# x turned on VectorE and through DRAM instead of on TensorE, sine and cosine in PSUM, and three banks for the matmul units

## The chip, the cores and the metric

One core of one Trainium2 chip. The metric is the device time of one execution in microseconds. The engines are TensorE (PE; its weight loads, PEld, overlap with its matmuls), VectorE (DVE), ScalarE (ACT), GpSimd (POOL), and SyncE (SP), whose queue issues the DMAs. SBUF is the working memory; PSUM holds matmul results in eight banks of 2 KB a partition.

## The reference

Eight batches, eight heads, 576 positions, head size 64; everything is fp32.

```
scores = q @ k.T / 8, masked:
  heads 0-3: 0 <= rel < 32
  heads 4-7: 0 <= rel < 128 and rel % 4 == 0
attn = softmax(scores); x = attn @ v          # laid out as [batch, 576, 512]
theta = x @ w_theta                           # [576, 512]
zr, zi = x * cos(theta), x * sin(theta)
y = w_tok_r @ zr + w_tok_i @ zi               # over the 576 positions
u = x + y
out = u + max(u @ w_ch, 0)
```

The kernel keeps fp32 accuracy by splitting each operand into a high part and a remainder (`hi`, `lo`) and adding three products.

## The kernel before

**Layout.** The banded attention is done per head pair (`NP` = 4 pairs a batch). Its result is x transposed: `xf[b, pr]`, 128 channels by 576 positions. Theta is computed in five stages of positions, `STS = (4, 0, 1, 2, 3)`; stage 4 has 64 positions, the others 128. Theta comes out with positions on the partitions, so sine and cosine have to be multiplied by x with positions on the partitions too. `natural` (L713) makes this x: four fp32 transposes on TensorE (L718) for each stage, into one PSUM bank (`pxs`), which is held until both the sine's and the cosine's multiply have read it.

**One head pair.** `scores` (L438): matmuls into two PSUM banks ("s"), mask and row maximum on VectorE (L406), exponentials on ScalarE (L501), scaling by the sums on GpSimd (L507). `turn` (L511): eight VectorE block transposes (L522) of the probabilities. `pv` (L600): matmul with v (L614) into the two-bank tile "v", copied out to `xf` by ScalarE (L578); `x_split` (L582) makes high and low parts of x (L590, L594, L596).

**One theta stage.** `theta` (L669): twelve matmuls (L682) into a bank of tag "t" or "s" (table `TP`). `trig` (L722) and `cosine` (L693): for stage 4 first a copy (L741) and an addition (L743); then rounding to whole turns (ACT L746), the fraction (DVE L748), sine (ACT L754), absolute value (ACT L695), cosine (ACT L697), the two multiplies by x (DVE L760 or L767 for the sine, L702 for the cosine), and for each product the high part (ACT L641) and the low part (POOL L643) in `zsplit`.

**Units.** Per batch 16 units: eight `token` units (27 matmuls each, L804; then DVE L782, ACT L785, POOL L787) and eight `chan` units (12 matmuls each, L834; then DVE L813). All take turns over the two banks of tag "m". The outputs leave by L819.

**Order.** For the first batches (0, most of 1) the order is written out by a planner (`Order`) with ranks and costs, and pinned. From then on `phase(b, nb)` (L841) issues batch b's units in program order with the next batch's attention, and the theta stages of `nb = b + 1` among the first five remaining channel units; the tables `S_AT`, `PV_AT`, `TURN_AT`, `TURN_TH` say at which unit each head pair's step is issued. In a phase the pairs 2 and 3 of batch nb and the pairs 0 and 1 of batch nb + 1 go through `scores` and `turn`. TensorE keeps program order; on the other engines the framework's scheduler sets the order when the kernel is built.

**PSUM.** s: two banks, v: two, t, x: one each, m: two. For batches 2 to 7 `natural` alternates between x and the first half of v:

```
XP = {4: "x", 0: "v", 1: "x", 2: "v", 3: "x"}
```

Of the kernel before, what the change touches and what calls it, by code (L numbers as in the profile page):

```python
# [8 lines left out]
F32 = mybir.dt.float32  # L9
# [27 lines left out]


FG0 = {4: ("zl2", "zl6"), 0: ("zl3", "zl7"), 1: ("zh3", "zh7")}
KORD = (0, 4, 1, 5, 2, 6, 3, 7, 8)  # L40
# [8 lines left out]
TURN_AT = {2: 0, 3: 1, 4: 5}  # L49
TURN_TH = {5: 1}  # L50
TH_AT = 7
NK = 9


# [5 lines left out]
class Order:  # L60
# [13 lines left out]
    def pin(self, ins):  # L74
        if self.live:
            self.tc.keep_in_program_order(ins)
# [73 lines left out]
def build(ctx, tc, qT, kT, vw, wth, wtk, wch, maskb, ident, identb, outT):  # L150
# [3 lines left out]
    sp = ctx.enter_context(tc.tile_pool(name="soft", bufs=2))  # L154
    xp = ctx.enter_context(tc.tile_pool(name="xu", bufs=2))
    hp = ctx.enter_context(tc.tile_pool(name="hilo", bufs=1))
    gp = ctx.enter_context(tc.tile_pool(name="trig", bufs=2))
    ps_s = ctx.enter_context(tc.tile_pool(name="ps_s", bufs=2, space=PSUM))
    ps_v = ctx.enter_context(tc.tile_pool(name="ps_v", bufs=1, space=PSUM))
# [36 lines left out]
    def give(tag, n):  # L196
        if od.live:
            signal(("free", tag, n))

    def bank(tag, name):  # L200
        if tag == "v":
            n = yield from take(tag, 1)
            return ps_v.tile([128, 2 * DM], F32, tag=tag, name=name)[:, :DM], (tag, n)
# [489 lines left out]
    def cosine(b, st, f, z, kt, key, rel):  # L693
        yield "ACT", act(DM)
        pin(nc.scalar.activation(f, f, AF.Abs))  # L695
# [4 lines left out]
        px, rx = pxs[b, st]  # L700
        yield "DVE", dve(DM)
        pin(nc.vector.tensor_tensor(z, px, f, op=ALU.mult))  # L702
        signal(key)
        if kt is not None:
            yield None, ("px", b, st)
            give(*rx)
            yield from zsplit(b, kt, z, rel)
        elif rel:
            give(*rel)

    pxs = {}

    def natural(b, st, cs):  # L713
        px, rx = yield from bank("mmxxm"[st] if b == 0 else "x" if b == 1 else XP[st], f"xn{b}_{st}")
        px = px[:cs.stop - cs.start]
        yield "PE", 430
        for c in range(NC):
            pe(nc.tensor.transpose(px[:, 128 * c:128 * c + 128], xf[b, c][:, cs], idt))  # L718
        pxs[b, st] = px, rx
        signal(("xn", b, st))  # L720

    def trig(b, st):  # L722
        cs = slice(128 * st, min(128 * st + 128, S))
        R = cs.stop - cs.start
        yield None, ("th", b, st) if b else ("th0", st, 3)
        pt, rt = ths.pop((b, st))
        go(natural(b, st, cs))
        if b == 0 and st in FG0:
            K, gt = (hp.tile([128, DM], F32R, tag=t, name=f"{n}{b}_{st}").bitcast(F32) for t, n in zip(FG0[st], "Kg"))
            K = K.bitcast(I32)[:R]  # L730
# [7 lines left out]
        th = pt[:R]  # L738
        if R == 64 and b > 0:
            yield "ACT", act(DM)  # L740
            pin(nc.scalar.copy(g, pt[R:]))  # L741
            yield "DVE", dve(DM)
            pin(nc.vector.tensor_tensor(g, th, g, op=ALU.add))  # L743
            th = g
        yield "ACT", act(DM)
        pin(nc.scalar.activation(K, th, AF.Copy, scale=I2PI))  # L746
# [7 lines left out]
        table(nc.scalar.activation(g, f, AF.Sin, scale=2 * math.pi))  # L754
        if R == 128:
            go(cosine(b, st, f, f, st, ("cos", b, st), rf))
            yield None, ("xn", b, st)
            px, rx = pxs[b, st]
            yield "DVE", dve(DM)
            pin(nc.vector.tensor_tensor(g, px, g, op=ALU.mult))  # L760
            signal(("px", b, st))
            yield from zsplit(b, 4 + st, g, rg)
        else:
            yield None, ("xn", b, st)
            px, rx = pxs[b, st]
            yield "DVE", dve(DM)
            pin(nc.vector.tensor_tensor(gt[128 - R:], px, g, op=ALU.mult))  # L767
            yield from cosine(b, st, f, g, None, ("cos", b, st), rf)
            give(*rx)
            yield from zsplit(b, 8, gt, rg)  # L770

    uh, ul = {}, {}
# [1 line left out]
    def residual(b, d, g, ps, rel):  # L774
# [12 lines left out]
        pin(nc.gpsimd.tensor_tensor(ul[b, d][:, ts], x[:, ts], uh[b, d][:, ts].bitcast(F32), op=ALU.subtract))  # L787
        signal(("u", b, d, g))

    def token(b, d, g):  # L790
        yield None, ("z", b, KORD[0])
        yield None, ("wtk", g, KORD[0] // 2)
        ps, rel = yield from bank("m", f"y{b}_{d}_{g}")
        ps = ps[:, :HS]
        cs = slice(128 * d, 128 * d + 128)
        n = 0
        for kt in KORD:
            yield None, ("z", b, kt)
            yield None, ("wtk", g, kt // 2)
            zh, zl = zs[b, kt]  # L800
            wh, wl = (w[:, HS * (kt % 2):HS * (kt % 2) + HS] for w in wtks[g, kt // 2])
            yield "PE", 369
            for l, r in ((zh, wh), (zh, wl), (zl, wh)):
                pe(nc.tensor.matmul(ps, l[:, cs], r, start=(n == 0), stop=(n == 3 * NK - 1)))  # L804
                n += 1
        signal(("tk", b, d, g))
        go(residual(b, d, g, ps, rel), RANK["evacuate"])
# [13 lines left out]
    def chan(b, e, g):  # L821
        yield None, ("u", b, 0, g)
        yield None, ("wch", 0)
        ps, rel = yield from bank("m", f"c{b}_{e}_{g}")
        ps = ps[:, :HS]
        cs = slice(128 * e, 128 * e + 128)
        ts = slice(HS * g, HS * g + HS)
        n = 0
        for c in range(NC):
            yield None, ("u", b, c, g)  # L830
            yield None, ("wch", c)
            yield "PE", 369
            for l, r in ((wchs[c][0], uh[b, c]), (wchs[c][0], ul[b, c]), (wchs[c][1], uh[b, c])):
                pe(nc.tensor.matmul(ps, l[:, cs], r[:, ts], start=(n == 0), stop=(n == 3 * NC - 1)))  # L834
                n += 1
        go(finish(b, e, g, ps, rel), RANK["evacuate"])
# [166 lines left out]
```

## Time and profile before

| | |
|---|---|
| median of 3 runs | 598.66 us (597.17 to 598.66) |
| profiled execution | 597.07 us |
| its span in the trace | 595.3 us |
| mean granted TensorE clock | 0.984 |
| busy share of the span | PE 96%, PEld 87%, DVE 61%, ACT 59%, POOL 37% |
| HBM | 57.41 MB read, 9.44 MB written |

The span is what the trace covers; the 1.8 us beside it are start and end of the execution. A row of the timeline has its start, its length, the engine, the line and operation, output and input, and in brackets the idle time ahead of it with what ended it. A row that groups instructions has the busy time, the mean length in ns of one, and the idle time ahead of them.

### The profile page before, as it was taken

To read this page: it belongs to the slowest core of one execution; us is meant where nothing else is said; L and a number is where in the kernel's file an instruction comes from. 1 tells how busy PE (TensorE), PEld (TensorE's weight loads), DVE (VectorE), ACT (ScalarE), POOL (GpSimd) and SP (SyncE) were. 2 spreads that over 40 slices of the span, in tenths; PEclk is the share of its full clock that TensorE was granted. 3 is DMA by queue.
4 is the path that set the end of the run, shared out by engine and by line. 5 is a ranking of instruction groups with operands and counts; after the bars stand their busy time and mean duration, and the time that the engine had idled before them with its cause. 6 is when DMAs were issued, how large, how long until landed. Compare 5 with 4: busy or idle time off the path is not lost.

```text
span 595.3 us, 14176 instructions
## 1 busy us (share of the span) xinstructions
PE 569.7 (96%) x5584; PEld 516.9 (87%) x5584; DVE 361.6 (61%) x1132; ACT 351.1 (59%) x939; POOL 222.4 (37%) x206
## 2 busy tenths in 40 slices
PE   5997898999999999999999999999999999999997
PEld 4744787979998899889998899989998899989997
DVE  3889888855765667465566567655665656445112
ACT  1498967687535955568553974468564785266110
POOL 2229854534322532326142442316324253315220
PEclk9999599999999999999999999999999999999999
DMA  8982347404650074302641054401742023001002
GB/s 303 398 339 61 121 160 246 142 1 141 182 160 3 2 241 142 101 2 89 197 139 62 1 181 151 154 1 40 231 142 73 0 81 100 1 1 53 28 1 81
DMA packets 26866, 67.76 MB, mean 114 GB/s; under 512 B 2992, under 2 KB 3248, under 8 KB 26800
## 3 DMA queue, kind: packets, MB, share of 16 engines
q1 hardware_dynamic: 26800, 66.86, 32.9%
q8 instruction: 44, 0.72, 0.5%
q14 instruction: 22, 0.18, 0.1%
HBM read 57.41 MB, written 9.44 MB: 112 GB/s over the span
## 4 chain that ended last, share of the span: by engine, by line
PE 49%; DVE 22%; ACT 21%; issue 3%; POOL 2%; DMA 2%; SPq 0%; ACTq 0%; DVEq 0%; POOLq 0%
PE y L804 27%; DVE pt L522 9%; PE c L834 8%; PE s L465 5%; ACT P L501 5%; PE o L614 4%; PE th L682 3%; ACT K L697 3%; ACT zh L641 3%; ACT g L754 2%; ACT K L695 2%; DVE P L406 2%; DVE K L702 2%; POOL P L507 2%; ACT L754 1%
## 5 line engine op out<-in xcount | busy, mean ns | idle before, releaser
L787 POOL TENSOR_TENSOR u<-x,u 128x288 fp32r<-128x288 f32 x64 | 54.9, 858 | 184.9 <-ACT u L785 162.2
L522 DVE STREAM_TRANSPOSE pt<-P 32x288 f32<-32x288 f32 x224 | 105.1, 469 | 21.1 <-POOL P L507 18.0
L834 PE MATMUL c<-u,late_wc 128*128 128x288 f32 x768 | 111.7, 296 | 0.8 <-DVE x L813 0.5
L834 PEld LDWEIGHTS c<-u,late_wc 128*128 128x128 f32 x768 | 106.2, 188 | 4.8 <-DVE x L813 2.0
L785 ACT CAST u<-x 128x288 fp32r<-128x288 f32 x64 | 27.5, 430 | 129.3 <-DVE x L782 129.3
L804 PE MATMUL y<-wtkh,zh 128*128 128x288 f32 x288 | 90.6, 315 | 1.1 <-ACT zh L641 1.1
L804 PE MATMUL y<-wtkh,zl 128*128 128x288 f32 x288 | 86.6, 301 | 3.7 <-POOL zl L643 3.7
L804 PE MATMUL y<-wtkl,zh 128*128 128x288 f32 x288 | 86.2, 299 | 0.0
L643 POOL TENSOR_TENSOR zl<-g,zh 128x512 fp32r<-128x512 f32 x40 | 52.6, 1316 | 79.1 <-ACT zh L641 66.7
L501 ACT ACTIVATE P<-P,mx 128x64 f32<-128x64 f32 x216 | 72.1, 336 | 16.8 <-DVE mx L495 16.8
L682 PE MATMUL th<-wthh,xh 128*128 128x512 f32 x224 | 76.3, 402 | 0.0
L782 DVE TENSOR_TENSOR x<-y,x 128x288 f32<-128x288 f32 x64 | 28.7, 450 | 66.8 <-PE y L804 64.0
L804 PE MATMUL y<-late_wt_b,zh 128*128 128x288 f32 x320 | 68.1, 297 | 0.0
L804 PE MATMUL y<-late_wt_a,zh 128*128 128x288 f32 x256 | 58.0, 308 | 2.7 <-DVE x L782 2.7
L804 PEld LDWEIGHTS y<-wtkh,zh 128*128 128x128 f32 x288 | 55.4, 192 | 4.8 <-ACT zh L641 2.3
L804 PEld LDWEIGHTS y<-wtkh,zl 128*128 128x128 f32 x288 | 55.3, 192 | 4.5 <-POOL zl L643 4.5
L804 PEld LDWEIGHTS y<-wtkl,zh 128*128 128x128 f32 x288 | 55.5, 193 | 0.3 <-issue 0.3
L643 POOL TENSOR_TENSOR zl<-K,zh 128x512 fp32r<-128x512 f32 x32 | 42.0, 1312 | 36.1 <-ACT zh L641 36.1
L507 POOL TENSOR_TENSOR P<-P,sm 128x576 f32<-128x576 f32 x32 | 37.5, 1172 | 43.8 <-ACT xh L590 19.3
L804 PEld LDWEIGHTS y<-late_wt_b,zh 128*128 128x128 f32 x320 | 51.4, 189 | 0.3
L682 PEld LDWEIGHTS th<-wthh,xh 128*128 128x128 f32 x224 | 42.1, 188 | 8.3
L804 PE MATMUL y<-late_wt_b,zl 128*128 128x288 f32 x160 | 47.3, 296 | 0.0
(103 smaller groups left out, 1110.0 us busy)
## 6 DMA issues: line engine op xcount, KB each, us to landing
q<-in_qT_dram SPq DMA_DIRECT2D x32, 576.0 KB, 4.2
va<-in_vw_dram SPq DMA_DIRECT2D x30, 320.0 KB, 3.2
out_dram<-x SPq DMA_DIRECT2D x32, 288.0 KB, 2.1
k<-in_kT_dram SPq DMA_DIRECT2D x28, 304.0 KB, 4.6
vb<-in_vw_dram SPq DMA_DIRECT2D x29, 256.0 KB, 3.4
st_wtk<-in_wtk_dram SPq DMA_DIRECT2D x8, 576.0 KB, 8.8
st_wth<-in_wth_dram SPq DMA_DIRECT2D x4, 512.0 KB, 9.8
st_wch<-in_wch_dram SPq DMA_DIRECT2D x4, 512.0 KB, 4.9
```

Of the source, the lines that this page charges most:

```text
L465: pe(nc.tensor.matmul(ps[64 * e:64 * e + 64, n - g0], q[:, qb], k[:, QB * qb:QB * qb + BW], start=not masked, stop=not masked or n == g1 - 1))
L501: table(nc.scalar.activation(P[:, n], P[:, n], AF.Exp, bias=mx[:, n:n + 1], scale=SCALE, accum_out=sm[:, n:n + 1]))
L507: pin(nc.gpsimd.tensor_tensor(P, P, sm.unsqueeze(2).to_broadcast([128, NJ, BW]), op=ALU.mult))
L522: pin(nc.vector.transpose(pmats[b, pr][k0:k0 + QB, :, hh, QB * e:QB * e + QB], P[p0:p0 + QB, :, QB * o:QB * o + QB]))
L614: pe(nc.tensor.matmul(ps[64 * hh:64 * hh + 64, BW * j:BW * j + BW], v[:, 64 * hh:64 * hh + 64], pmats[b, pr][:, j, hh], start=True, stop=T ...
L643: pin(nc.gpsimd.tensor_tensor(lo, z, hi.bitcast(F32), op=ALU.subtract))
L682: pe(nc.tensor.matmul(pt, l, r, start=(n == 0), stop=(n == 3 * NC - 1)))
L782: pin(nc.vector.tensor_tensor(x[:, ts], ps, x[:, ts], op=ALU.add))
L785: pin(nc.scalar.copy(uh[b, d][:, ts], x[:, ts]))
L787: pin(nc.gpsimd.tensor_tensor(ul[b, d][:, ts], x[:, ts], uh[b, d][:, ts].bitcast(F32), op=ALU.subtract))
L804: pe(nc.tensor.matmul(ps, l[:, cs], r, start=(n == 0), stop=(n == 3 * NK - 1)))
L834: pe(nc.tensor.matmul(ps, l[:, cs], r[:, ts], start=(n == 0), stop=(n == 3 * NC - 1)))
```

## The change

It concerns batches 2 to 7, and the units of batches 1 to 7.

- x with positions on the partitions is no longer made by TensorE. `x_turn` transposes the 32 x 32 blocks of each `xf[b, c]` (128 x 576) on VectorE, issued after the pair's `pv`. What is left is a shuffle of whole blocks: `x_store` writes them with four DMAs to a DRAM tile (runs of 512 bytes), issued at unit 4, and `x_load` reads the rows back with five DMAs into the same SBUF space, issued at unit 6. The multiplies read this x (`by_x`).
- The cosine is written to PSUM (two halves of "v", alternating over the stages), the sine into the theta bank that it was computed from; the multiplies read it there.
- The units use three banks in turn (m, m, x) instead of two.
- The context's scratch for software DMAs is set to 1024 bytes.

```diff
-XP = {4: "x", 0: "v", 1: "x", 2: "v", 3: "x"}
+STORE_AT, LOAD_AT = 4, 6
...
     def cosine(b, st, f, z, kt, key, rel):
...
-        table(nc.scalar.activation(f, f, AF.Sin, scale=-2 * math.pi, bias=halfpi[:f.shape[0]]))
+        cs = f
+        if b > 1 and COS_PSUM:
+            if st == STS[0]:
+                cos_at[b] = yield from bank("v", f"cos{b}")
+            cs = cos_at[b][0][:f.shape[0], DM * (STS.index(st) % 2):][:, :DM]
+        table(nc.scalar.activation(cs, f, AF.Sin, scale=-2 * math.pi, bias=halfpi[:f.shape[0]]))
...
-        pin(nc.vector.tensor_tensor(z, px, f, op=ALU.mult))
+        by_x(b, st, z, cs)
...
+    def x_turn(b, c):
+        if c == 0:
+            t = cp.tile([128, 5 * DM], F32, tag="xn", name=f"xq{b}")[:, :NC * S]
+            xq[b] = t.rearrange("p (a c s) -> p a c s", c=NC, s=QB)
+        pin(nc.vector.transpose(xq[b][:, :, c], xf[b, c].rearrange("p (a s) -> p a s", s=QB)))
+
+    def x_store(b):
+        xq[b], t = dp.tile([S, DM], F32, tag="xd", name=f"xd{b}"), xq[b]
+        to = xq[b].rearrange("(a s) (g f) -> s a g f", s=QB, g=4)
+        for g in range(4):
+            pin(nc.sync.dma_start(to[:, :, g], t[QB * g:QB * g + QB].rearrange("p a c s -> p a (c s)")))
+
+    def x_load(b):
+        xn = cp.tile([128, 5 * DM], F32, tag="xn", name=f"xn{b}").rearrange("p (a d) -> p a d", d=DM)
+        for st in STS:
+            R = 64 if st == 4 else 128
+            pin(nc.sync.dma_start(xn[:R, st], xq[b][128 * st:128 * st + R]))
+            xns[b, st] = xn[:R, st].rearrange("p (g c d) -> p c g d", g=4, c=NC)
+
+    def by_x(b, st, z, f):
+        if b > 1:
+            z, f = (t.rearrange("p (c g d) -> p c g d", c=NC, g=4) for t in (z, f))
+            pin(nc.vector.tensor_tensor(z, xns[b, st], f, op=ALU.mult))
+        else:
+            pin(nc.vector.tensor_tensor(z, pxs[b, st][0], f, op=ALU.mult))
 
     def natural(b, st, cs):
+        if b > 1:
+            return
...
-        table(nc.scalar.activation(g, f, AF.Sin, scale=2 * math.pi))
+        sn = th0 if b > 1 and SIN_PSUM else g
+        table(nc.scalar.activation(sn, f, AF.Sin, scale=2 * math.pi))
...
+    def unit_bank(b, n):
+        return "mmx"[n % 3] if b else "m"
...
     def phase(b, nb):
...
+            for p in range(NP):
+                if PV_AT[p] == n and nb > 1:
+                    x_turn(nb, p)
+            if n == STORE_AT and nb > 1:
+                x_store(nb)
+            if n == LOAD_AT and nb > 1:
+                x_load(nb)
             n += 1
```

More of the change, by code (lines that the diff above doesn't have):

```diff
@@ L39 @@
 FG0 = {4: ("zl2", "zl6"), 0: ("zl3", "zl7"), 1: ("zh3", "zh7")}
+COS_PSUM, SIN_PSUM = True, True
 KORD = (0, 4, 1, 5, 2, 6, 3, 7, 8)
@@ L156, in build @@
     hp = ctx.enter_context(tc.tile_pool(name="hilo", bufs=1))
+    dp = ctx.enter_context(tc.tile_pool(name="dram", bufs=2, space=bass.MemoryType.DRAM))
     gp = ctx.enter_context(tc.tile_pool(name="trig", bufs=2))
@@ L202, in bank @@
             n = yield from take(tag, 1)
-            return ps_v.tile([128, 2 * DM], F32, tag=tag, name=name)[:, :DM], (tag, n)
+            return ps_v.tile([128, 2 * DM], F32, tag=tag, name=name), (tag, n)
         pl, bufs = banks[tag]
@@ L696, in cosine @@
         yield "ACT", act(DM) + 90
[L697 removed]
+        cs = f
[4 more added lines that the diff above has]
+        table(nc.scalar.activation(cs, f, AF.Sin, scale=-2 * math.pi, bias=halfpi[:f.shape[0]]))
         signal(("sin", b, st))
         yield None, ("xn", b, st)
[L700 removed]
         yield "DVE", dve(DM)
[L702 removed]
+        by_x(b, st, z, cs)
         signal(key)
         if kt is not None:
[L705 to L706 removed]
+            if b < 2:
+                yield None, ("px", b, st)
+                give(*pxs[b, st][1])
             yield from zsplit(b, kt, z, rel)
@@ L709, in cosine @@
             give(*rel)
-    pxs = {}
+    pxs, cos_at = {}, {}
+    xq, xns = {}, {}
+    def x_turn(b, c):
[20 more added lines that the diff above has]
+            pin(nc.vector.tensor_tensor(z, pxs[b, st][0], f, op=ALU.mult))
     def natural(b, st, cs):
-        px, rx = yield from bank("mmxxm"[st] if b == 0 else "x" if b == 1 else XP[st], f"xn{b}_{st}")
+        if b > 1:
+            return
+        px, rx = yield from bank("mmxxm"[st] if b == 0 else "x", f"xn{b}_{st}")
         px = px[:cs.stop - cs.start]
@@ L737, in trig @@
         g = gt[:R]
-        th = pt[:R]
+        th = th0 = pt[:R]
         if R == 64 and b > 0:
@@ L757, in trig @@
             yield None, ("xn", b, st)
-            px, rx = pxs[b, st]
             yield "DVE", dve(DM)
-            pin(nc.vector.tensor_tensor(g, px, g, op=ALU.mult))
+            by_x(b, st, g, sn)
+            if b > 1:
+                give(*rt)
             signal(("px", b, st))
@@ L764, in trig @@
             yield None, ("xn", b, st)
-            px, rx = pxs[b, st]
             yield "DVE", dve(DM)
-            pin(nc.vector.tensor_tensor(gt[128 - R:], px, g, op=ALU.mult))
+            by_x(b, st, gt[128 - R:], sn)
             yield from cosine(b, st, f, g, None, ("cos", b, st), rf)
-            give(*rx)
+            if b < 2:
+                give(*pxs[b, st][1])
             yield from zsplit(b, 8, gt, rg)
@@ L792, in token @@
         yield None, ("wtk", g, KORD[0] // 2)
-        ps, rel = yield from bank("m", f"y{b}_{d}_{g}")
+        ps, rel = yield from bank(unit_bank(b, NC * g + d), f"y{b}_{d}_{g}")
         ps = ps[:, :HS]
@@ L823, in chan @@
         yield None, ("wch", 0)
-        ps, rel = yield from bank("m", f"c{b}_{e}_{g}")
+        ps, rel = yield from bank(unit_bank(b, NC * (2 + g) + e), f"c{b}_{e}_{g}")
         ps = ps[:, :HS]
@@ L989 @@
     host = _arrays({n: _np.asarray(a) for n, a in inputs.items()})
-    nc = _bacc.Bacc("TRN2", target_bir_lowering=False, num_devices=1)
+    nc = _bacc.Bacc("TRN2", target_bir_lowering=False, num_devices=1,
+                     dynamic_dma_scratch_size=1024)
     arrays, args = {}, []
```

## The prediction

> **What bounds the kernel now.** I read the page first (busy shares, groups, DMA), then the length of one batch, then the chain of waits, and last the engines' timelines through one batch. In steady state one "phase" runs the token and channel units of batch b while batch b+1 is prepared; five phases (b = 1 to 5) are alike, and b = 6 has no softmax work two batches ahead of it any more.
>
> ```profile
> PE 569.7 (96%) x5584; PEld 516.9 (87%) x5584; DVE 361.6 (61%) x1132; ACT 351.1 (59%) x939; POOL 222.4 (37%) x206
> ...
> 344.89:413.78 68.89, 67.83 (x677) 63.05 (x677) 42.93 (x155) 42.23 (x121) 24.34 (x24) 1.00 0.32 105
> ...
> 317.00:345.00 28.00, 27.76 (x171) 24.75 (x171) 16.35 (x37) 20.62 (x47) 10.41 (x10) 1.00 0.01 1
> ```
>
> The columns of the stage rows are: stretch, length, then busy us of PE, PEld, DVE, ACT, POOL, the clock, the DMA share. A phase takes about 68.7 us and TensorE shows 67.8 of it busy, so at first sight only TensorE counts: what is taken off it is gained. The chain of waits says otherwise:
>
> ```profile
> 353.33 1.20 PE o L614 x36
> ...
> 386.47 3.10 ACT P L501 x18
> 390.73 1.17 POOL P L507
> 395.80 0.69 DVE g L743
> ...
> 413.78 3.46 PE c L834 x24
> ```
>
> From 353.33 to 413.78, 60 us of that 69 us phase, the chain never touches TensorE. It goes: exponentials (L501) on ScalarE, scaling by the sums (L507) on GpSimd, block transposes of the probabilities (L522) on VectorE, the next pair's mask and maximum, its exponentials, and so on through four head pairs; then the trigonometry of the five theta stages, up to 413.78, where a channel unit on TensorE has to wait for a PSUM bank that VectorE empties (L813) behind its trigonometry. In the other phases the chain shown runs over TensorE in the first half and joins this one at the last pair, so the two loops have nearly the same length. That is my main reading: **two loops tie**, and the change shortens only one of them directly.
>
> How long is the second loop by itself? One turn of it, by VectorE's timeline:
>
> ```profile
> 288.43 3.86 DVE L522 STREAM_TRANSPOSE pt<-P 32x288 f32<-32x288 f32 x8
> ...
> 323.04 3.85 DVE L522 STREAM_TRANSPOSE pt<-P 32x288 f32<-32x288 f32 x8 [1.58 <-POOL P L507]
> 326.92 0.68 DVE L743 TENSOR_TENSOR g<-th,g 64x512 f32<-64x512 f32 x1
> ...
> 357.10 3.37 DVE L522 STREAM_TRANSPOSE pt<-P 32x288 f32<-32x288 f32 x7
> ```
>
> and ScalarE's rows between:
>
> ```profile
> 327.63 0.63 ACT L746 ACTIVATE K<-g 64x512 int32<-64x512 f32 x1 [5.11 <-DVE g L743]
> ...
> 335.18 0.63 ACT L641 CAST zh<-K 128x512 fp32r<-128x512 f32 x1 [0.28 <-DVE K L702]
> ...
> 347.38 0.62 ACT L641 CAST zh<-K 128x512 fp32r<-128x512 f32 x1 [0.76 <-DVE K L702]
> 347.98 0.62 ACT L641 CAST zh<-g 128x512 fp32r<-128x512 f32 x1
> 348.62 1.28 ACT L501 ACT_TABLE_LOAD   x1
> 350.76 0.35 ACT L501 ACTIVATE P<-P,mx 128x64 f32<-128x64 f32 x1 [0.86 <-DVE mx L495]
> ...
> 353.86 0.43 ACT L785 CAST u<-x 128x288 fp32r<-128x288 f32 x1
> ```
>
> 288.43 to 357.10 is 68.67. The pieces: first to last probability transposes 38.46 (288.43 to 326.89); to the first rounding 0.74 (327.63); the trigonometry 20.97 (to 348.60); the table load 1.30 (to 349.90); a gap of 0.86, which is the only place where TensorE's scores set the pace; exponentials 3.10 (350.76 to 353.86); then 3.24 to the next transposes. Without the gap the loop is 67.8. Theta of stage 4 is copied out long before: ScalarE then sits idle 5.11 us because L743 is queued behind L522 on VectorE.
>
> In a sentence by itself: the Trainium skill, page "Trainium Kernel Development and Optimization", section "Best Practices", says that matmul busy time is not the measure of how near TensorE is to its limit, and that the busy share of the weight loads is; by that the engine stands at 87% and not at 96%.
>
> **The change part by part.** *Removed from TensorE:* the four fp32 transposes of x for each of five stages in batches 2 to 7, 30 stages in all. The undisturbed price stands in the last theta stretch:
>
> ```profile
> 524.43 1.58 PE c L834 x12
> 526.01 0.44 PE xn L718 x4
> 526.45 2.74 PE th L682 x12
> ```
>
> 0.44 a stage, 2.2 us a phase, 13.2 us in all. *Third bank:* units no longer wait for one of two banks. The waits on TensorE's weight loads from 207 to 560:
>
> ```profile
> PEld y L804 <- DVE x L782: 3.2, 4, 1.0
> ...
> PEld c L834 <- DVE x L813: 2.0, 5, 0.4
> PEld xn L718 <- PE c L834: 1.4, 4, 0.4
> ```
>
> Together 6.6 us over five phases, 1.3 a phase, which goes with the transposes' own bank waits. TensorE's own loop falls from 68.7 to 68.7 - 2.2 - 1.3 = 65.2. That is a floor and not the time, because the other loop stands at 67.8.
>
> *Added to VectorE:* four block transposes a phase, 128 x 576 each. The trace has only L522's form:
>
> ```profile
> L522 DVE STREAM_TRANSPOSE pt<-P 32x288 f32<-32x288 f32 x224 | 105.1, 469 | 21.1 <-POOL P L507 18.0
> ```
>
> If time goes by columns, 2 x 0.469 = 0.94; if four times the partitions and twice the columns cost no more than one such instruction, 0.47. I take 0.94, since the 288 columns at 0.469 already stand at 1.6 ns a column. VectorE has room for 3.8 us (43 of 69 busy); the question is what queues behind each. An x transpose can run once the copy of x out of PSUM (L578) is done, so their places are:
>
> ```profile
> 295.70 0.46 DVE L782 TENSOR_TENSOR x<-y,x 128x288 f32<-128x288 f32 x1 [2.40 <-PE y L804]
> 303.56 0.69 DVE L596 TENSOR_TENSOR xh<-x,xh 128x512 fp32r<-128x512 f32 x1
> 309.53 1.19 ACT L578 COPY x<-o 128x576 f32<-128x576 f32 x1
> 311.66 3.85 DVE L522 STREAM_TRANSPOSE pt<-P 32x288 f32<-32x288 f32 x8 [1.90 <-POOL P L507]
> ```
>
> The second falls into the idle 2.40 before 295.70: nothing. The fourth is ready at 310.72 and fits into the 1.90 before 311.66: nothing. The first becomes ready just before the 288.43 transposes; with TensorE ahead, the mask work beside it moves earlier, so I take 0, at most 0.94. The third lands among the splits near 303.5 with the next pair's mask and maximum, its exponentials and its transposes queued behind, and no slack up to the trigonometry: 0.94. Sum on the loop 0.94, bounds 0 and 1.88.
>
> *x through DRAM:* four stores, then five loads that wait for them, on SP's queue.
>
> ```profile
> q1 hardware_dynamic: 26800, 66.86, 32.9%
> ...
> out_dram<-x SPq DMA_DIRECT2D x32, 288.0 KB, 2.1
> 311.80 0.33 SPq L218 DMA_DIRECT2D q<-in_qT_dram  x1
> ...
> 344.90 4.34 SPq L819 DMA_DIRECT2D out_dram<-x  x4
> 330.24 0.68 DVE L767 TENSOR_TENSOR g<-xn,g 64x512 f32<-64x512 f32 x1 [1.26 <-ACT g L754]
> ```
>
> Behind the waiting stores on SP stand at most the loads of the next pair, issued at 311.80 and so no later than now; after them come the output stores of 344.90, and the DMA share from 317 to 345 is 0.01, so nothing collides. The transfer of 1.18 MB goes out in runs of 512 bytes, 2304 of them, 144 on each of 16 engines. Lower bound: the 2.1 of an output store. Upper: each run costs as much as a mean packet of the queue, 0.329 x 595.3 x 16 / 26800 = 0.117 us, so 16.8. I take 8. The loads, 1.18 MB again but in runs of 2048 bytes, I put at 5: above the 2.1 of one 288 KB store, below four of these in a row, 8.4. From 311.7 that is 325, before the first use at 330.24; with the store's upper bound 333.5, 3.3 late. Nothing on the path, bounds 0 and 3.3. If x came late, VectorE would stall at L767 with the whole trigonometry behind it.
>
> *Sine and cosine in PSUM:* the multiplies still read one operand from PSUM and one from SBUF, so L760 and L702 keep their 0.68. ScalarE writes PSUM in ten instructions a phase. No row shows such a write; the nearest shows the reading side:
>
> ```profile
> L695 ACT ACTIVATE K<-K 128x512 f32<-128x512 f32 x32 | 20.2, 631 | 0.9
> L746 ACT ACTIVATE K<-th 128x512 int32<-128x512 f32 x32 | 18.7, 585 | 2.7 <-PE th L682 2.5
> ```
>
> So 0 to 46 ns each, 0 to 0.46 a phase; I take 0.2. The Trainium skill, page "ScalarE: Activation LUTs", section "Step-by-step: what each stage is for", says PSUM is the quicker destination for ScalarE, without a figure; no run so far shows it, and by it the sum would take the 0.46 end. The theta bank is held until the sine is multiplied: the second half of the next scores then waits for stage 3's L760, which in the old order ended at 347.94. That is no loss while the loop ends there anyway, but it stops TensorE from running further ahead than one scores block.
>
> The smaller DMA scratch adds no instruction.
>
> *Order of the multiplies:* today L702 (cosine) goes ahead of L760 (sine) although the sine is ready 1.3 us sooner, and ScalarE waits 0.27 three times and 0.76 once for it (1.57 a phase). With x already in SBUF nothing ties the sine's multiply to TensorE. The order on VectorE is a scheduler's, so I take 1.0 of the 1.57. Of the gap of 0.86 I take half, 0.43, as the last L813 stand ahead of the masks.
>
> **The sum.** A steady phase: 68.67 + 0.94 - 1.0 - 0.2 - 0.43 = 67.98, so -0.7, times five = -3.5. The phase of b = 6 has no softmax loop and runs on TensorE: -2.2, of which I leave 0.5 for z parts coming late: -1.7. Units alone at the end: no change. Together -5.2 on the profiled 597.07 (span 595.3): 591.9. The runs' median is 1.6 above the profiled one: **593.5**.
>
> **Rivals.** *TensorE is the bound after all* (0.18). If all of 0.86, 1.57 and 0.46 comes and no x transpose is on the loop, it is 65.8, beside the floor 65.2: 5 x -2.9 - 2.2 = -16.7, so 582 in the runs' terms; if L743 also gets ahead of L522, the floor: 579. For: 67.8 of 68.7 busy. Against: the 5.11 us wait, a VectorE order that holds in all steady phases. *Nothing gained* (0.17). The order stays, only the gap goes and the x transpose eats it: 68.67 - 0.86 + 0.94 = 68.75; 597.3 with the last phase. *VectorE takes it back: slower* (0.15). Two x transposes stand ahead of L522 and the masks, no wait goes: 68.67 + 1.88 - 0.43 = 70.1; 5 x 1.45 - 1.7 = +5.6, so 604. It decides from about 0.9 us a phase on the loop that nothing repays. For: no slack between 303.5 and 327. Against: idle spots of 2.40 and 1.90. *x comes late* (0.07): 3.3 a phase at the upper bound, 5 x 2.6 - 1.7, about 610. For: small runs; against: an idle DMA.
>
> **How the numbers follow.** My forecast has 0.43, its own range 588 to 597. The range 580 to 604 leaves out the far ends of the first and the last two rivals. This kernel's measurement tells 0.3%, 1.8 us. Faster by that: most of the forecast (0.38), the TensorE case (0.18), a little of "nothing" (0.04): 0.60. Same: 0.12 + 0.05 = 0.17. Slower: 0.15 + 0.07 and a tail: 0.23.
>
> **What would show it.** Right: no L718 rows after batch 1; phases near 68; TensorE idle ahead of scores, released by the sine's multiply; the chain on L522, L501 and the trigonometry in every steady phase. The x transposes show their own rate and place. Wrong: phases of 65 to 66 with TensorE on the whole chain (the loops did not tie, or the order broke the second); L743 or L767 waiting for a DMA; ScalarE writes of sine slower than 630 ns.

## The result, and the profile after

The changed kernel takes **583.52 us** (median of 4 runs, 583.05 to 584.45), the kernel before 598.11 on the same chip: a ratio of 0.976, 95% interval [0.974, 0.978], or 14.6 us less. The forecast was 593.5. The profiled execution took 583.05, its span 581.3, at a mean granted TensorE clock of 0.988 (0.984 before).

The page of the changed kernel: busy time by engine, and the chain's shares by engine. Line numbers have moved: transposes of the probabilities L522 are L525 now, exponentials L501 are L504, rounding L746 is L787, multiplies by x L748, x transposes L729.

```profile
PE 553.6 (95%) x5464; PEld 502.7 (86%) x5464; DVE 378.0 (65%) x1156; ACT 344.3 (59%) x939; POOL 222.6 (38%) x206
...
DVE 32%; PE 29%; ACT 26%; POOL 6%; issue 4%; DMA 2%; SPq 1%; ACTq 0%; DVEq 0%; POOLq 0%
```

TensorE still shows 95% busy, yet it holds only 29% of the chain. Stage rows (stretch, length, then busy us of PE, PEld, DVE, ACT, POOL, clock, DMA share, GB/s): first a steady phase and the last phase of the kernel before, then the same two of the changed one.

```profile
279.95:348.62 68.67, 67.91 (x684) 63.07 (x680) 42.72 (x155) 42.19 (x121) 24.35 (x24) 1.00 0.32 106
485.93:550.34 64.41, 64.41 (x607) 60.87 (x607) 32.28 (x96) 36.53 (x85) 23.17 (x23) 1.00 0.13 43
```

```profile
277.99:344.27 66.28, 65.28 (x658) 60.86 (x658) 45.38 (x158) 40.91 (x120) 24.36 (x23) 1.00 0.47 145
474.16:536.44 62.28, 62.28 (x587) 58.69 (x587) 35.64 (x101) 36.34 (x86) 24.58 (x24) 1.00 0.29 87
```

A steady phase lost 2.4 us and the last one 2.13; 5 x 2.4 + 2.1 = 14.1 is the whole gain (the two profiled executions are 14.0 apart). One turn of the second loop, by VectorE's timeline and then ScalarE's, of the changed kernel:

```profile
284.29 3.87 DVE L525 STREAM_TRANSPOSE pt<-P 32x288 f32<-32x288 f32 x8
...
319.02 3.85 DVE L525 STREAM_TRANSPOSE pt<-P 32x288 f32<-32x288 f32 x8 [1.58 <-POOL P L510]
...
350.56 0.94 DVE L525 STREAM_TRANSPOSE pt<-P 32x288 f32<-32x288 f32 x2
```

```profile
323.62 0.63 ACT L787 ACTIVATE K<-g 64x512 int32<-64x512 f32 x1 [5.11 <-DVE g L784]
...
342.21 0.62 ACT L644 CAST zh<-K 128x512 fp32r<-128x512 f32 x1 [0.75 <-DVE K L748]
342.85 1.28 ACT L504 ACT_TABLE_LOAD   x1
344.27 0.35 ACT L504 ACTIVATE P<-P,mx 128x64 f32<-128x64 f32 x1
```

By the prediction's own pieces:

| piece of one turn | before | after | difference | predicted |
|---|---|---|---|---|
| first to last probability transposes | 38.46 | 38.58 | +0.12 | +0.94 |
| to the first rounding | 0.74 | 0.75 | +0.01 | 0 |
| trigonometry | 20.97 | 19.21 | -1.76 | -1.2 |
| table load | 1.30 | 1.30 | 0 | 0 |
| gap before the exponentials | 0.86 | 0.14 | -0.72 | -0.43 |
| exponentials to the next transposes | 6.34 | 6.29 | -0.05 | 0 |
| sum | 68.67 | 66.27 | -2.40 | -0.7 |

All three terms missed on the same side. The third **x transpose** of a phase on VectorE, the group of all of them, and the first one as it stands in the chain of waits:

```profile
294.85 0.76 DVE L729 STREAM_TRANSPOSE xq<-x 128x576 f32<-128x576 f32 x1
295.54 3.83 DVE L525 STREAM_TRANSPOSE pt<-P 32x288 f32<-32x288 f32 x8
```

```profile
L729 DVE STREAM_TRANSPOSE xq<-x 128x576 f32<-128x576 f32 x24 | 18.6, 773 | 9.9 <-ACT x L581 9.9
```

```profile
282.01 0.78 DVE xq L729
```

0.77 each instead of the 0.94 taken. The third stands directly ahead of the next probability transposes, as forecast. From this pair's exponentials to the next pair's (289.45 to 302.19) it is 12.74, against 12.08 before (294.12 to 306.20): +0.66. But the pair ahead of it is shorter, 11.46 instead of 12.01. ScalarE's rows there, before and after:

```profile
293.25 0.43 ACT L785 CAST u<-x 128x288 fp32r<-128x288 f32 x1 [5.99 <-DVE x L782]
293.59 0.63 ACT L578 COPY x<-o 128x576 f32<-128x576 f32 x1
294.12 0.35 ACT L501 ACTIVATE P<-P,mx 128x64 f32<-128x64 f32 x1
```

```profile
287.37 0.64 ACT L581 COPY x<-o 128x576 f32<-128x576 f32 x1 [4.68 <-DMA k<-in_kT_dram]
289.11 0.43 ACT L828 CAST u<-x 128x288 fp32r<-128x288 f32 x1 [1.11 <-DVE x L825]
289.45 0.35 ACT L504 ACTIVATE P<-P,mx 128x64 f32<-128x64 f32 x1
```

Before, the copy of x out of PSUM stood between the unit's cast and the exponentials, though ScalarE had idled 5.99 us ahead of them. Now it runs first, in that idle time, and 0.55 us comes off the loop. That repays most of the third transpose.

The first x transpose is on the chain too, in every steady phase. It costs nothing against the kernel before, because VectorE waited in that place for the next pair's scores (0.84 us ahead of the masks at 286.50). From the exponentials to the transposes of the probabilities it is 6.30 us now (277.99 to 284.29) and was 6.32 (282.11 to 288.43).

**x through DRAM** came in time. SyncE's issues of the changed kernel, and the first use of x:

```profile
307.57 3.78 SPq L736 DMA_DIRECT2D xd<-xq  x4
...
315.41 2.50 SPq L742 DMA_DIRECT2D xn<-xd  x5
```

```profile
326.82 0.68 DVE L748 TENSOR_TENSOR g<-xn,th 64x512 f32<-64x512 f32 x1 [0.85 <-ACT th L796]
```

A load takes 4.9 us to land (median), so the last is there at about 322.8, 4 us before the first use. That use waits for the sine (`th L796`), not for x.

**Writes to PSUM.** ScalarE's cosine and sine, before (first fence) and after; the columns are busy us, mean ns, idle before:

```profile
L697 ACT ACTIVATE K<-K,halfpi 128x512 f32<-128x512 f32 x32 | 23.1, 722 | 0.8
L754 ACT ACTIVATE g<-K 128x512 f32<-128x512 f32 x32 | 20.1, 629 | 3.8 <-DVE K L748 3.2
```

```profile
L705 ACT ACTIVATE cos<-K,halfpi 128x512 f32<-128x512 f32 x24 | 16.5, 687 | 0.1
L796 ACT ACTIVATE th<-K 128x512 f32<-128x512 f32 x24 | 14.3, 597 | 1.9 <-DVE K L789 1.9
```

35 and 32 ns less each, 0.33 us a phase over ten. The Trainium skill, page "ScalarE: Activation LUTs", section "Step-by-step: what each stage is for", says that ScalarE is faster to PSUM than to SBUF; these rows agree.

The largest share of the 1.76 is **ScalarE's order**. Its waits for VectorE or GpSimd in the trigonometry fell only from 1.58 us (0.28, 0.27, 0.27, 0.76) to 1.27 (0.27, 0.25, 0.75). What changed is how closely its instructions follow each other. Two stretches of it, before and after:

```profile
336.43 0.63 ACT L754 ACTIVATE g<-K 128x512 f32<-128x512 f32 x1
337.10 0.63 ACT L695 ACTIVATE K<-K 128x512 f32<-128x512 f32 x1
```

```profile
338.69 0.60 ACT L796 ACTIVATE th<-K 128x512 f32<-128x512 f32 x1
339.22 0.61 ACT L644 CAST zh<-K 128x512 fp32r<-128x512 f32 x1
339.73 0.63 ACT L698 ACTIVATE K<-K 128x512 f32<-128x512 f32 x1
340.26 0.61 ACT L644 CAST zh<-g 128x512 fp32r<-128x512 f32 x1
```

Sine and absolute value of one stage use one tile in turn and start 0.67 us apart; absolute value and cosine 0.66. The two casts and the next sine started 0.60 and 0.65 apart (335.18, 335.78, 336.43), right behind VectorE's two multiplies and fraction, which run end to end (334.45, 335.06, 335.66). With another stage's instruction between two that depend on each other they start 0.51 to 0.53 apart. In the trigonometry of a phase 3 starts before and 14 after come within 0.56 us of the one ahead. 11 x 0.15 would be 1.6 us; writes and waits leave 1.76 - 0.33 - 0.31 = 1.1 for it. That split is worked out from the rows; no run changes ScalarE's order alone. The Trainium skill, page "ScalarE: Activation LUTs", section "What ACT_TABLE_LOAD costs", gives about 93 ns by which activations in a row overlap; here that is so (0.60 busy, 0.51 apart) only where the neighbours do not share a tile.

The changed kernel's chain also runs over GpSimd's low parts inside the trigonometry, in four of the five steady phases. The chain of the kernel before holds none of them there:

```profile
333.23 3.82 POOL zl L646 x3
```

What a faster low part would give was not tried.

### The profile page after: what moved, and what is told of

Same layout as the page of the kernel before. It is cut to its first block, busy times and chain, and to the rows that moved or that the text cites. A ratio compares the mean times of both kernels' runs of the same rounds, so it can differ in the third digit from the quotient of the medians.

```text
span 581.3 us, 13989 instructions
## 1 busy us (share of the span) xinstructions
PE 553.6 (95%) x5464; PEld 502.7 (86%) x5464; DVE 378.0 (65%) x1156; ACT 344.3 (59%) x939; POOL 222.6 (38%) x206
## 4 chain that ended last, share of the span: by engine, by line
DVE 32%; PE 29%; ACT 26%; POOL 6%; issue 4%; DMA 2%; SPq 1%; ACTq 0%; DVEq 0%; POOLq 0%
DVE pt L525 14%; PE y L850 13%; ACT P L504 10%; PE c L880 7%; PE th L685 4%; DVE P L409 4%; POOL zl L646 3%; DVE xh L599 2%; POOL P L510 2%; ACT zh L644 2%; PE s L468 2%; ACT K L698 2%; ACT K L787 2%; ACT cos L705 2%; ACT th L796 2%
## 5 line engine op out<-in xcount | busy, mean ns | idle before, releaser
L525 DVE STREAM_TRANSPOSE pt<-P 32x288 f32<-32x288 f32 x224 | 104.9, 468 | 12.5 <-POOL P L510 8.9
L880 PE MATMUL c<-u,late_wc 128*128 128x288 f32 x768 | 108.9, 295 | 0.0
L685 PE MATMUL th<-wthh,xh 128*128 128x512 f32 x224 | 75.0, 396 | 5.4 <-DVE g L748 5.2
L504 ACT ACTIVATE P<-P,mx 128x64 f32<-128x64 f32 x216 | 72.1, 335 | 13.1 <-DVE mx L498 12.4
L685 PEld LDWEIGHTS th<-wthh,xh 128*128 128x128 f32 x224 | 42.0, 188 | 15.2 <-PE c L880 4.8
L581 ACT COPY x<-o 128x576 f32<-128x576 f32 x32 | 29.6, 924 | 28.7 <-PE o L617 23.9
```

The costliest lines, as they stand in the source:

```text
L504: table(nc.scalar.activation(P[:, n], P[:, n], AF.Exp, bias=mx[:, n:n + 1], scale=SCALE, accum_out=sm[:, n:n + 1]))
L525: pin(nc.vector.transpose(pmats[b, pr][k0:k0 + QB, :, hh, QB * e:QB * e + QB], P[p0:p0 + QB, :, QB * o:QB * o + QB]))
L581: pin(nc.scalar.copy(dst, src))
L685: pe(nc.tensor.matmul(pt, l, r, start=(n == 0), stop=(n == 3 * NC - 1)))
```

## The experiments

Theory 1 is the prediction's: TensorE's loop and the second loop (VectorE, ScalarE, GpSimd) nearly tie, and the change shortens the second by its order of multiplies, PSUM writes and gap, the first by transposes and bank waits. The rivals are that TensorE was the only bound, and that the third bank, or sine ahead of cosine, alone explains the gain. NOSYNC in the diffs stands for a dependency of order only. The period is that of the third steady phase, from one table load of the exponentials to the next; "against" is the median less 583.52 (the first four and the last five rows) or less the kernel before on the same chip (the middle four). The kernel before took 598.11 us where the changed one was timed, and 597.06 to 598.01 on the chips of these runs.

| version | median us | against | period |
|---|---|---|---|
| changed, units on two banks | 591.00 | +7.5 | 67.78 |
| changed, sine and cosine in SBUF | 594.73 | +11.2 | 68.63 |
| changed, cosine's multiply first | 588.01 | +4.5 | 67.20 |
| changed, half of TensorE's transposes back | 588.63 | +5.1 | 67.01 |
| before, sine's multiply first | 598.60 | +0.7 | 68.93 |
| before, one x a batch | 597.01 | 0.0 | 68.42 |
| the same, third bank | 591.54 | -6.1 | 68.32 |
| before, last transposes spread | 594.23 | -2.8 | 67.97 |
| changed, second x transpose twice | 584.37 | +0.9 | 66.27 |
| changed, third twice | 580.11 | -3.4 | 65.57 |
| changed, third twice, order held | 586.04 | +2.5 | 66.70 |
| changed, order held | 583.88 | +0.4 | 66.26 |
| changed, last transposes spread | 578.01 | -5.5 | 65.03 |

### Undoing one part of the change

**Two banks.**

```diff
     def unit_bank(b, n):
-        return "mmx"[n % 3] if b else "m"
+        return "m"
```

> The changed kernel with its third bank undone: the units of batches 1 to 7 take turns over the two banks of tag m again. Theory 1 (the loop over VectorE, ScalarE and GpSimd sets a steady phase at 66.28 us, TensorE has about 1 us of idle time in it): the bank waits come back, 0.6 to 1.0 us a phase, and fall mostly into that idle time: 0 to +2 us on 583.5. Theory 2 (TensorE sets the end): 5.2 us of bank waits come back: +4 to +5.

591.00 us, ratio to before 0.9887 [0.9863, 0.9911]: 7.5 us worse than the changed kernel, more than either theory gave. TensorE's weight loads over the whole span:

```profile
PEld c L880 <- DVE x L859: 6.8, 5, 1.4
PEld y L850 <- DVE x L825: 6.6, 5, 1.5
```

Both waits are absent from the changed kernel. The gap before the exponentials is 0.96 instead of 0.14, and ahead of it the masks wait for TensorE's scores (348.73, 0.28 us), which come behind units that waited 1.13 for a bank. The stretch from the exponentials' table load to the sine's is 49.6 us instead of 48.3, so the head pairs pay for a bank that VectorE empties late. The third bank works on the second loop and not on TensorE's alone.

**Sine and cosine in SBUF.**

```diff
-COS_PSUM, SIN_PSUM = True, True
+COS_PSUM, SIN_PSUM = False, False
```

> The changed kernel with sine and cosine written to SBUF again, so that both operands of the multiplies by x lie in SBUF. Theory 1: ScalarE loses 10 x 33 ns a phase (599 to 632, 687 to 723), and the multiplies, which run beside GpSimd's low parts, stretch as the SBUF-only subtraction at L599 does (1.64 us beside GpSimd, 0.68 without): 1 to 3 us a phase, +5 to +15 us. Theory 2: 0, since TensorE does the same work and its theta banks come free sooner.

594.73 us, ratio to before 0.995 [0.9931, 0.9969]. The multiplies by x in this run:

```profile
L748 DVE TENSOR_TENSOR g<-xn,g 128x512 f32<-128x512 f32 x24 | 29.6, 1235 | 4.3 <-ACT g L796 4.2
...
L748 DVE TENSOR_TENSOR K<-xn,K 128x512 f32<-128x512 f32 x24 | 26.7, 1111 | 5.0 <-ACT K L705 4.4
```

With both operands in SBUF a multiply takes 1.1 to 1.2 us; with one in PSUM it took 0.68. These are means. Two single ones of one phase, while GpSimd is idle and while its low parts run:

```profile
333.96 0.68 DVE L748 TENSOR_TENSOR g<-xn,g 128x512 f32<-128x512 f32 x1
...
337.19 1.71 DVE L748 TENSOR_TENSOR g<-xn,g 128x512 f32<-128x512 f32 x1
```

Once x has left PSUM, putting sine and cosine there is not an extra: without it 11.2 of the 14.6 us are gone. The Trainium skill, page "GPSIMD Engine Reference", section "8. Key points", says that GpSimd contends with VectorE instructions that have two SBUF inputs; this agrees.

**Cosine's multiply first**, as before the change:

```diff
-    xq, xns = {}, {}
+    xq, xns, by_cos = {}, {}, {}
...
-            pin(nc.vector.tensor_tensor(z, xns[b, st], f, op=ALU.mult))
+            ins = nc.vector.tensor_tensor(z, xns[b, st], f, op=ALU.mult)
+            if st < 4 and (b, st) in by_cos:
+                tc.add_manual_dep(ins.ins, by_cos[b, st].ins.name, NOSYNC, reason="cosine first")
+            by_cos[b, st] = ins
```

> The changed kernel with one thing held: on VectorE the cosine's multiply of a stage goes ahead of the sine's, as in the kernel before. Theory 1: the trigonometry, now 19.20 us, gets most of the 1.57 us of waits back: +1.0 to +1.6 a phase, +5 to +8 us. Theory 2: 0.

588.01 us, ratio 0.9823 [0.9793, 0.9853]: 0.92 us a phase, a little under theory 1. The first exponential of this run:

```profile
348.93 0.35 ACT L504 ACTIVATE P<-P,mx 128x64 f32<-128x64 f32 x1 [0.78 <-DVE mx L498]
```

The gap before the exponentials is back, 0.78 instead of 0.14. With 0.32 more from the sine's table load to the exponentials' that is the 0.92 (0.04 come off elsewhere): the order of the multiplies acts mostly through this gap. The masks wait for nothing here; they follow the sine's multiply and two additions.

**Half of TensorE's transposes back**, into the theta bank ahead of its matmuls, unused:

```diff
+        if b > 1:
+            w = min(128, S - 128 * st)
+            for c in range(2):
+                pe(nc.tensor.transpose(pt[:w, 128 * c:128 * c + 128], xf[b, c][:, 128 * st:128 * st + w], idt))
```

> The changed kernel with two fp32 transposes of x put back on TensorE ahead of every theta stage of batches 2 to 7; they write into the theta bank and theta overwrites them, so nothing waits for them and nothing uses them. Half of what the change took off: 0.22 a stage, 1.1 us a phase, 6.6 in all. Theory 1: 1.0 of each 1.1 falls into TensorE's idle time in the five steady phases, all of it shows in the last: +1 to +3. Theory 2: +6 to +7.

588.63 us, ratio 0.9846 [0.9827, 0.9865]; 0.73 us a phase, between the two theories. The stage row:

```profile
277.58:344.59 67.01, 66.56 (x669) 61.92 (x666) 45.73 (x160) 41.42 (x120) 24.32 (x24) 1.00 0.48 144
```

TensorE's work grew by 66.56 - 65.28 = 1.28 and the period by 0.73. The difference came out of its wait for the theta bank (1.0 us in this phase of the changed kernel, 0.4 here). The 0.73 shows as 0.35 in the trigonometry and 0.42 in the gap before the exponentials, now 0.56 (0.04 come off elsewhere). So TensorE has 0.5 to 0.6 us of room after the change: the two loops still nearly tie, one step lower.

### One part alone, in the kernel before

**Sine's multiply first:**

```diff
...
+        if (b, st) in sins_at:
+            tc.add_manual_dep(ins.ins, sins_at[b, st].ins.name, NOSYNC, reason="sine first")
...
```

> The kernel before with one thing held: on VectorE the sine's multiply of a stage goes ahead of the cosine's in batches 2 to 7. Theory 1 (two loops tied): the second loop falls by 1.0 to 1.6 us a phase, TensorE's stays near 68: -0.5 to -3 us on 598. Rival 3 (the order of the multiplies is most of the gain by itself): -5 to -8.

598.60 us, ratio 1.0016 [1.0001, 1.0032]; theory 1 had -0.5 to -3. Its stage row:

```profile
279.04:347.97 68.93, 67.85 (x678) 63.04 (x678) 43.24 (x154) 41.66 (x120) 24.29 (x24) 1.00 0.32 106
```

The trigonometry did shrink, from 20.97 to 20.55 us, and nothing came of it: the gap before the exponentials grew from 0.86 to 1.52. Ahead of it the masks wait for TensorE's scores, here as in the kernel before, whose row is this:

```profile
349.13 0.22 DVE L406 CUSTOM_DVE_ANT_0 P<-s,mskb 128x64 f32<-128x64 f32 x1 [0.28 <-PE s L465]
```

The scores come no sooner than TensorE's last 24 unit matmuls let them.

**One x a batch**, which takes work off TensorE:

```diff
     def natural(b, st, cs):
+        if b > 1 and st != STS[0]:
+            pxs[b, st] = pxs[b, STS[0]]
+            return
+        if b > 1:
+            cs = slice(0, 128)
...
```

> The kernel before, with one turned tile of x in each of the batches 2 to 7: positions 0 to 127 are turned on TensorE and all five stages multiply by that tile, so four of the five sets of turns are left out, with them the multiplies by the right x in stages 1 to 4; the cosine's multiply is held ahead of the sine's as it stands before. This takes about 1.76 us a phase off TensorE and nothing off the second loop but what of the 0.86 gap TensorE alone had caused. Two loops that tie (theory 1): -2 to -4.5 us, that is 0.4 to 0.9 a phase. TensorE alone sets the period (rival): -9 us, all of the 1.76 in each of five phases.

597.01 us, ratio 0.9983 [0.9964, 1.0002]: nothing that can be told, at most 2.1 us by the interval, where theory 1 expected 2 to 4.5. Stage row, TensorE's wait in it, and the exponentials:

```profile
279.73:348.15 68.42, 66.05 (x662) 61.36 (x660) 42.67 (x154) 41.72 (x120) 24.34 (x24) 1.00 0.32 106
```

```profile
PE c L844 <- DVE x L823: 1.9, 1, 1.9
```

```profile
350.73 0.35 ACT L501 ACTIVATE P<-P,mx 128x64 f32<-128x64 f32 x1 [1.29 <-DVE mx L495]
```

TensorE has 1.86 us less to do and spends it waiting for a unit's bank. The phase is 0.25 shorter. TensorE as the only bound falls. The run did not relieve TensorE alone, though: the scheduler's order changed with it, and the trigonometry is 20.27, 0.70 less. The gap took that up. It grew to 1.29, and the masks wait 0.28 for the scores here too. So TensorE's scores do set the gap, as the prediction read it, but not by TensorE's load.

What sets them is the same in the kernel before, with sine first and here. VectorE empties a unit's bank inside its trigonometry, TensorE's last 24 unit matmuls start (344.89, 344.91, 344.85), and the first exponential follows 5.87, 5.86 and 5.88 us later, behind these matmuls, the scores and the masks. This path crosses from one loop to the other over the two banks. What lies beside it, the end of the trigonometry or TensorE's transposes, can shrink without a gain.

**The same with the third bank**, the one x kept in the output's bank (the diff beside that of the run above):

```diff
-XP = {4: "x", 0: "v", 1: "x", 2: "v", 3: "x"}
+XP = {4: "v"}
...
-        ps, rel = yield from bank("m", f"y{b}_{d}_{g}")
+        ps, rel = yield from bank("mmx"[(NC * g + d) % 3] if b else "m", f"y{b}_{d}_{g}")
...
-        ps, rel = yield from bank("m", f"c{b}_{e}_{g}")
+        ps, rel = yield from bank("mmx"[(NC * (2 + g) + e) % 3] if b else "m", f"c{b}_{e}_{g}")
```

> The kernel before with one turned tile of x in each of the batches 2 to 7, as in the run that took 1.76 us a phase off TensorE (four of five sets of turns left out, stages 1 to 4 multiply by the wrong x), and besides that tile kept in the output's bank and the units of batches 1 to 7 on three banks in turn; the order of the instructions on each engine is that run's. What it tells apart is what the third bank is worth when TensorE has room and nothing else of the change is made. Third bank as the prediction sized it (it ends TensorE's waits for banks, and lets the scores come on time; the second loop keeps its length but for the 0.76 before the exponentials): 67.6 to 67.8 a phase, -3 to -4 us against that run. Banks emptied in VectorE's order hold TensorE in the second loop (the +1.5 a phase that the changed kernel lost on two banks): 66.7 to 67.2 a phase, -6 to -9 us. Units' banks play no part before the change: 0.

591.54 us, ratio 0.9889 [0.9861, 0.9918]. By medians 5.5 us less than without the bank, by profiled executions 2.5 (594.82 and 592.31); the four later periods are 67.8 to 68.3. By the profiles the five phases give 1.4 us together and the last one 1.3, less than either expectation; by the medians it lies between them. The second loop by itself is near 68 us in the old order, and the bank, worth 1.5 us a phase after the change, has little to give under it. At the end of the phase a gap of 0.77 stays, and VectorE's rows show its cause:

```profile
346.34 0.68 DVE L767 TENSOR_TENSOR g<-xn,g 128x512 f32<-128x512 f32 x1
346.94 0.81 DVE L823 SCALAR_TENSOR_TENSOR x<-c,x 128x288 f32<-128x288 f32 x2
347.66 0.21 DVE L406 CUSTOM_DVE_ANT_0 P<-s,mskb 128x64 f32<-128x64 f32 x1
```

The masks follow without a pause behind the sine's multiply and two additions; TensorE's scores are already there (346.19 to 347.46). In the changed kernel the sine's multiply is done before the cosine's, and that gap is the one that came back with cosine's multiply first.

**Last transposes spread.** The eight transposes of the last pair (L522) stand in one block of 3.85 us, with L743 queued behind them; here two of them follow each stage's fraction:

```diff
-TURN_TH = {5: 1}
+TURN_TH = {5: 4}
...
+            if pr == 1 and (b - 1, i // 2) in fracs:
+                tc.add_manual_dep(ins.ins, fracs[b - 1, i // 2].ins.name, NOSYNC, reason="late turn")
```

> The kernel before, with nothing changed but the place of the last pair's eight transposes of probabilities on VectorE: two behind the fraction of each theta stage, as in the version of the changed kernel where this gave 5.5 us. Theory 1 (the second loop then gets ahead and TensorE, busy 67.8 of 68.7 us in a phase, is left as the bound): -3 to -5 us, no more than the 0.9 a phase that TensorE idles. Were the second loop the only bound, as in the changed kernel: -5 to -8 us.

594.23 us, ratio 0.9938 [0.9916, 0.9959]; -2.8 us, just short of theory 1's -3 to -5. The phase is 67.97, 0.70 shorter, with TensorE busy for 67.44 of it, and the chain is 71% TensorE's. This is the run that relieves the second loop alone, and it shows how near the two loops were.

### The price of the x transposes

The second or the third of the four block transposes is made twice:

```diff
+        if c == 2:
+            nc.vector.transpose(xq[b][:, :, c], xf[b, c].rearrange("p (a s) -> p a s", s=QB))
```

> The changed kernel with the second x transpose of each batch done twice (0.77 us more on VectorE a phase, in a place with 1.29 us of idle time behind it). Theory 1: 0 to +0.5. Rival 4 (VectorE's load as such counts): +3.9.

> The changed kernel with the third x transpose of each batch done twice (0.76 us more on VectorE a phase, ahead of the next pair's masks, with nothing idle behind it up to the trigonometry). Theory 1: +0.76 in each of five phases, +3 to +4. Theory 2 (TensorE sets the end): 0. Rival 4 (load as such): +3.9 as for the second.

The second doubled (c == 1): 584.37 us, ratio 0.9779 [0.9755, 0.9803], period unchanged. It is free. The third doubled: 580.11, ratio 0.9711 [0.9688, 0.9734], faster. That is not the price of anything, as VectorE's rows show:

```profile
320.13 1.43 DVE L525 STREAM_TRANSPOSE pt<-P 32x288 f32<-32x288 f32 x3 [1.67 <-POOL P L510]
321.60 0.68 DVE L786 TENSOR_TENSOR g<-th,g 64x512 f32<-64x512 f32 x1
322.31 2.41 DVE L525 STREAM_TRANSPOSE pt<-P 32x288 f32<-32x288 f32 x5
```

The scheduler's order changed: stage 4's addition (L786 here) slipped between the last pair's transposes, and the trigonometry begins sooner. So the run was repeated with that addition held behind all eight transposes, beside a control with the same hold and nothing doubled:

```diff
...
+            if b + 1 in lasts:
+                tc.add_manual_dep(ins.ins, lasts[b + 1].ins.name, NOSYNC, reason="after the transposes")
...
```

> The changed kernel with the third block transpose of x made twice in each of the batches 2 to 7, and the addition of theta's last stage held behind all eight transposes of the last pair, where the changed kernel has it. Theory 1 (this transpose stands on VectorE's path from the last exponentials to the next sines): +0.77 us a phase, +3 to +4 us against the changed kernel with the same hold. Rival (it lies in VectorE's idle time): 0.

> The changed kernel with the same hold of the addition and nothing doubled. Its order on VectorE is the changed kernel's around the last transposes, so 0 (within 1 us) against it by each theory; it is what the doubled one is compared with.

586.04 (ratio 0.9805 [0.9786, 0.9824]) against 583.88 (0.9772 [0.975, 0.9793]): 2.2 us, 0.44 a phase, short of the 3 to 4 expected. The pair with the doubled transpose takes 0.68 longer, and the next one makes up 0.23. The third is on the loop, at a little over half its length. Between the two doubled runs, 580.11 and 586.04, the place of stage 4's addition is worth 5.9 us.

### A version that beats both

The same spreading of the last transposes, in the changed kernel (the diff is that of the kernel before):

> The changed kernel with the eight block transposes of the last head pair (L525) held back: two behind the fraction (L789) of each of the stages 0 to 3, instead of all eight ahead of L784. Theory 1: the trigonometry starts up to 4.4 us sooner in each steady phase, the loop over VectorE and ScalarE falls below TensorE's, and TensorE sets the phase at its busy 65.3: 5 x -1.0, about 578.5. Theory 2 (TensorE sets the end already): 0.

**578.01 us** (577.66 to 578.08), ratio to before 0.9671 [0.9653, 0.9689]. Its stage row, and the chain by engine:

```profile
273.91:338.94 65.03, 65.03 (x658) 60.83 (x656) 45.48 (x158) 41.98 (x121) 24.29 (x24) 1.00 0.50 148
```

```profile
PE 80%; DVE 9%; ACT 5%; DMA 2%; issue 2%; POOL 1%; SPq 0%; DVEq 0%; ACTq 0%; POOLq 0%
```

TensorE has no idle time left in the phase and the chain is TensorE's. This is the floor that the prediction gave for TensorE's own loop, 65.2.

## Why the prediction was right and wrong

**Two loops tie: held.** Relieving the second loop alone gave 0.70 a phase and then TensorE held it (594.23). Less work for TensorE gave 0.25 a phase (597.01), a shorter end of the trigonometry nothing (598.60); the change took 2.4. What the sum left out is the path over the two banks that ties the loops to each other. The prediction's own chain shows it, where a channel unit waits at 413.78 for a bank behind the trigonometry. The rival "TensorE is the bound after all" named the right size (582) with the wrong cause: its chain should have been TensorE's, and it holds 29%. Its sum for the second loop, 65.8 if everything comes, was the better one.

**The step that failed is the sum for the second loop**, -0.7 a phase where -2.40 came:

- *x transposes, +0.94 taken.* The place was right (the third) and 0.66 showed there; each takes 0.77 instead of 0.94. That is 0.28 of the error of 0.82. The rest is a gain of 0.55 that was not looked for: the copy of x ahead of the exponentials left the loop.
- *Order of the multiplies and PSUM writes, -1.2 taken, -1.76 measured.* The sum is nearer than its terms. Sine ahead of cosine gives 0.32 in the trigonometry (taken: 1.0), the writes up to 0.33 (taken: 0.2). The rest, about 1.1, was missed: ScalarE's own instructions close up. The prediction counted the waits shown in brackets; the 0.1 to 0.15 us that a start loses behind a neighbour it depends on stands in no bracket.
- *The gap, -0.43 taken, -0.72 measured.* It was put down to TensorE's scores, of which half was to go. Two things hold it, and either alone keeps it. On two banks the scores come late (0.86 before, 0.96 in the changed kernel with two banks). On three banks the scores are there in time, but in the old order the masks stand behind the sine's multiply (0.78). Only with both gone is it 0.14.

**The third bank** was counted for TensorE's loop only, 1.3 a phase there and nothing in the sum. Putting it back to two cost 1.5 a phase, of which 0.82 is the gap. It belongs to both loops, since VectorE empties the banks in its own order. Its place in the second loop's sum was a term put at nothing.

**What held:** -1.7 for the last phase was -2.13; x through DRAM in time (15.2 us from the first store's issue to the last landing where 13 were taken, and 4.0 us before the first use instead of 5.2); the second x transpose shown free, the fourth not on the chain, and the first on it but at no cost. The longer hold of the theta bank became TensorE's new wait, about 1.0 us once in a phase, though ahead of theta's matmuls and not of the scores:

```profile
PE th L685 <- DVE g L748: 5.2, 5, 1.2
```

**What stays open.** The parts' losses when undone (1.5, 2.4, 0.92, 0.73 a phase) add up to far more than 2.4; each is a loss of the whole arrangement, so no split of the 14.6 us by parts is given. Why the scheduler put ScalarE's copy and casts into the better places was not tried apart from the change.

## What to carry to other kernels

Where two loops tie, test each alone before sizing a change, and look for what passes between them: here less work for TensorE gave 0.25 us a phase, less for the second loop 0.70, and the change, which relieved both and added a bank between them, 2.4. Size a loop on an in-order engine by start-to-start distances and not by busy times and bracketed waits alone, and expect that a changed order by the scheduler is worth as much as the work moved (0.55 us a phase for one copy, 5.9 us in all for one addition that slipped ahead). A buffer count is a term of every loop that fills or empties the buffer.

## What the hardware showed that was not expected

- VectorE's multiplies with both operands in SBUF take 1.11 and 1.24 us on average beside GpSimd's work, up to 1.71, and 0.68 while it is idle; with one in PSUM they take 0.68.
- ScalarE's 128 x 512 instructions of 0.60 to 0.63 us start 0.51 to 0.53 us apart when neighbours share no tile and wait for nothing, 0.66 to 0.67 apart when they share one.
- A VectorE block transpose of 128 x 576 fp32 takes 0.77 us, one of 32 x 288 takes 0.47: four times the partitions and twice the columns for 1.65 times the time.
